# A planned transformer-layer kernel in a new order: DMAs planned with eight lanes, copies of value rows planned after the second x load

## The chip, the cores and the metric

The kernel runs on one core of one Trainium2 chip. The core has five engines with a queue each: TensorE (PE, matmuls), VectorE (DVE), ScalarE (ACT), GpSimd (POOL) and SyncE (SP, which here issues DMAs). The metric is device time in microseconds (us) of one execution. Times below come from three runs of the kernel and from one profiled execution of it.

## The reference

For x of 2048 tokens by 448 channels, bf16:

```python
xn = _layernorm(x, axis=-1)
s = _A_ref(xn, A_wqkv, A_wo)                              # attention
g = _silu(_B_ref(xn, B_w1, B_b1, B_w2, B_b2))             # 448 -> 1792, gelu, -> 448
return x + s * g
# attention: 16 heads of 28; a query at position p sees p, p-2, ..., p-14 (8 keys, step 2)
# softmax over these 8, weighted sum of their values, heads joined, times wo
```

## The kernel before, in words

**Tiles.** Tokens are kept as even ones and odd ones, 16 tiles of 128 tokens, in four chunks of four tiles. The work of a chunk is: load x, statistics (`stats`, L434 and L438 on DVE), reciprocal deviation (`rstds`: for tiles 0 to 3 on ACT and DVE, for later ones two POOL instructions, L455 and L456, over two or four tiles at once), normalised rows (`norm`, L468 on DVE; L482 doubles 64 columns), their transposition (chunk 0 on PE, L492; later chunks by a DMA transpose from SP, `dma_T`, L391), then projections to q and k (`qk_cols`: L583 in chunk 0, L580 later), to values (`vproj`: L619 in chunk 0, inside L510 later) and the first product of the feed-forward part (`ff1`, L510) with its gelu on ACT (L662). Attention is done in nine visits of some 228 queries: scores (L808), exp on ACT (L818), a mask on DVE or POOL (L825), the weighted sum (L841), and four DVE instructions that divide (L852 to L866). The second product `ff2` (L510, at the end L752), its gate (L775 to L785) and the product with wo (L510, at the end L926) close the work with a sum, and SP writes the rows out (L945).

**Copies of value rows.** A visit needs its 128 value rows at other partitions than those where `vproj` left them. `values` (L629) copies them by two or more DMAs issued from POOL (`dma_sb`, L383 to L387), 52 in all, into one of six buffers v0 to v5.

**Last 128 columns of the feed-forward part.** For chunks 1 to 3 they are made by unused columns of the q and k products: `spread` (L1003 to L1018) lays the weights out once, and `moved` (L558) copies 8 rows at a time from qT and kT to a tile hx by DMAs from SP (L567), 16 for a chunk. One gelu on ACT (L673) closes each.

**Halves and nops.** Most products are done by `pair` (L522): two products share the array, 64 rows by 64 columns a matmul. The first half issues 16 matmuls, the second half 12, in swapped places. Between them stands a nop on POOL (L535): it waits for the first half, and the second half waits for it. So a second half on PE can't start before POOL's queue has come to its nop.

**The order.** Nothing is scheduled on the chip. `_Plan` holds a list of tasks, each with an engine, a cost in us, the tasks before it and a priority. `run` (L98) goes through them as a list scheduler with that model of the time and fixes one order for every engine, and `emit` writes the program in that order. DMAs are tasks on an engine named "DMA" of the model, after the issuing instruction. Priorities are tables (`PRIO`, `LATER`, L284 to L306). The order is all that the plan decides: the semaphore waits of the program come from the data that its instructions read and write.

**Lanes.** Every DMA of the program signals its landing on one of eight semaphores, in turn: eight for those that SP and ACT issue, in one sequence, and eight for those of POOL. A DMA is issued only when the one that had its semaphore before has landed. The program before has these waits in it; the plan before knows nothing of them. For example the eighth value copy waits for the landing of b1's load, the ninth for that of the first value copy, and so on.

**POOL's queue around 9 to 20 us, before** (what follows "nop" is what it lets go):

```
copies v0 v0 v0 | nop 1 | copies v1 v2 v1 v2 v2 v2 (the last two wait for a lane) | nop 2 | copy v3 (lane)
| nop 3 | copy v4 (lane) | rstd of tiles 4, 5 | nop 4 | rstd of tiles 6, 7 | nop 5 | copy v5 | nop 6 | copy v3
| three spread copies (L1006) | ...
```

**ACT's and SP's queues, before.** SP issues all early loads: x of tiles 0, 2, 3, the weights of q, k and v, then the first half of w1 (one large, two small DMAs), x of tiles 4 to 7, the second half of w1. Later come four transposes, 16 copies to hx, eight transposes, and so on. ACT issues x of tile 1 early and, between its evacuations of PSUM, x of tiles 8 to 11, the first half of w2, x of tiles 12 to 15 and the second half of w2; in the program before, 8 of SP's hx copies stand between the first and the last of these four in the sequence of lanes.

Of the kernel before, what the change touches and what calls it, by code (L numbers as in the profile page):

```python
# [13 lines left out]
HOP = 0.10  # L14
# [2 lines left out]
SWITCH = 0.095  # L17
BLOCK, FETCH = 128, ((0.0, 5.4), (25.0, 4.0))
SAME = 20
HOPS = ("POOL", "POOL")  # L20
MASK_ON = (("DVE", "POOL"), (0.4, 1.2))

# [9 lines left out]

class _Task:
    __slots__ = ("eng", "cost", "deps", "fn", "prio", "take", "give", "slots",
                 "start", "end", "on", "ndep", "users", "tail", "seq", "table", "limit", "mode", "pairs")


class _Plan:
# [5 lines left out]
        self.tasks = []  # L44

    def add(self, eng, cost, fn, deps=(), prio=0, take=(), give=(), tail=0.0, table=(), limit=None,
            mode=128, pairs=1):
        t = _Task()
        t.eng = eng if isinstance(eng, tuple) else (eng,)
        t.cost = cost if isinstance(cost, tuple) else (cost,) * len(t.eng)  # L50
        t.deps = [d for d in deps if d is not None]
        t.fn, t.prio, t.give, t.tail, t.table, t.limit = fn, prio, give, tail, table, limit
        t.mode, t.pairs = mode, pairs
        t.take = {}
        for p in take:
            t.take[p] = t.take.get(p, 0) + 1
        t.slots = {}
        t.start = t.end = None
        t.on = None
        t.users = []  # L60
        t.seq = len(self.tasks)
        self.tasks.append(t)
        for p in t.take:
            if p.fifo is not None:
                p.fifo.append(t)
        return t

    def _at(self, t, e, free):
        at = free.get(e, 0.0)
        for p, n in t.take.items():  # L70
            if len(p.free) < n or p.fifo and p.fifo[0] is not t:
                return None
            at = max(at, sorted(p.free)[n - 1][0] + HOP)
        if t.table and self.table not in t.table:
            at += TABLE
        for d in t.deps:
            at = max(at, d.end - d.tail if d.on == e else d.end + HOP)
        if e == "PE" and t.mode != self.mode:
            at = max(at, free.get(e, 0.0) + SWITCH)
        return at  # L80
# [17 lines left out]
    def run(self):  # L98
# [4 lines left out]
        free = {}  # L103
        self.table = None
        self.mode, self.issued, self.block = 128, 33, -9.0
        ready = [t for t in self.tasks if not t.ndep]
        order = []
        while ready:
            cand = []
            for t in ready:  # L110
                ways = []
                for e, c in zip(t.eng, t.cost):
                    at = self._at(t, e, free)
                    if at is not None:
                        ways.append((at + (c if len(t.eng) > 1 else 0.0), at, e, c))
                if ways:
                    _, at, e, c = min(ways)
                    cand.append((at, t, e, c))
            if not cand:
                raise RuntimeError("the plan is stuck: " + str([(t.seq, t.eng, t.fn.__qualname__) for t in ready[:20]]))  # L120
            first = min(cand, key=lambda k: k[0])
            near = [k for k in cand if k[2] == first[2] and k[0] <= first[0] + SLACK]
            at, t, e, c = min(near, key=lambda k: (-k[1].prio - self.same(k[2], k[1]),
                                                   k[0], k[1].seq))
            if t.limit is not None and at > t.limit:
                t.fn, c = None, 0.0
            t.on, t.start = e, at
            if e == "PE" and t.fn is not None:
                self.mode = t.mode
                c = self.fetched(at, c, t.pairs)  # L130
            if t.table and self.table not in t.table:
                self.table = t.table[0]
            free[e] = at + c
            t.end = at + c + t.tail
            for p, n in t.take.items():
                got = sorted(p.free)[:n]
                for g in got:
                    p.free.remove(g)
                t.slots[p] = [g[1] for g in got]
                if p.fifo is not None:  # L140
                    p.fifo.pop(0)
            for p, owner, i in t.give:
                p.free.append((t.end, owner.slots[p][i]))
            ready.remove(t)
            order.append(t)
            for u in t.users:
                u.ndep -= 1
                if not u.ndep:
                    ready.append(u)
# [24 lines left out]
def kernel(  # L174
# [87 lines left out]
    def ring(name, n, shape, dt=BF16, fifo=False):  # L262
# [19 lines left out]


    PRIO = {  # L284
        "spread": (-1,),
        "gather": (119, 152.5, 45.5,),
        "qk": (-31, -42, 39.5, 35.5, 17.5, 190, 183.5, 22.5, 124.5, 86, 32, 107.5, 156.5, 104, 142,
            157.5,),
        "values": (52, 145, 24.5, 138.5,),
        "attn": (194, 183, 206, 72.5, 26.5, 16, 45, 78.5, 28,),  # L290
        "ff1": (-56, 2.5, 37.5, 66, 54, 197.5, -17, 14.5, 34.5, 201.5, 19.5, 164, 129.5, 79, 151.5,
            65.5, 16.5, 76, 11.5, 152.5, -15, 138.5, 10, 15.5, 77, 146.5, 142, 70,),
        "gelu": (162, -60, 34.5, 95,),
        "ff2": (2, 101, 1.5, 41, 71, 136, 20, 77, 182, 70.5, 27, 184, 49.5, 6, 17, 16,),
        "final": (20.5, 94.5, 6.5, 113.5, 193.5, 87, 133.5, 38.5, 53.5, 85.5, 0, 20, 5.5, 16, 51.5,
            105,),
        "norm": (50, 8, 97.5, 178.5, 71, 126, 152.5, 51.5, 198.5, 162.5, 89.5, 102, 99, -14.5, 17.5,
            114,),
        "loads": (10, 50, 84.5, 70, 92,),
        "stats": (207.5, 159.5, 110, 199.5, 114.5, 85, 105, 153, 8.5, 4, 95, 95.5, 207, 174, 144.5,  # L300
            85,),
        "turn_x": (27, 181, 74.5, 10.5, 190, 177, 105.5, 75.5, 134.5, 92, 15.5, 88.5, 145, 9.5, 135,
            111,),
        "move_v": (16, 19, 126.5, 47, 183, 104, 197, 195, 126,),
    }
    LATER = {"swap": 92, "qk": 55.5, "v": 108.5, "gelu": 178, "exp": 94.5, "mask": -33.5, "pv": -0.5, "recip": 64, "os": 186, "y": 120.5, "tanh": 33.5, "g": 8, "sg": 78, "o": 146.5}  # L306

    plan = _Plan()

# [64 lines left out]
    def dma(eng, dst, src, kb, prio, deps=(), issue=0.5, rate=350.0, tail=1.7, pieces=1):  # L374
        def fn(_):
            {"SP": nc.sync, "ACT": nc.scalar, "POOL": nc.gpsimd}[eng].dma_start(dst, src)
        a = plan.add(eng, issue, fn, [t_on] + list(deps), prio)
        for _ in range(pieces - 1):
            a = plan.add("DMA", kb / rate / pieces, lambda _: None, [a], prio - 100)
        return plan.add("DMA", kb / rate / pieces, lambda _: None, [a], prio - 100 * (pieces > 1), tail=tail)  # L380


    def dma_sb(dst, src, deps, prio, take=(), give=()):  # L383
        def fn(k):
            nc.gpsimd.dma_start(dst(k), src())  # L385
        a = plan.add("POOL", 0.55, fn, deps, prio, take=take)
        return a, plan.add("DMA", 0.4, lambda _: None, [a], prio, give=give, tail=2.2)  # L387

    def dma_T(dst, src, deps, prio, give, n=1, issue=1.45):
        def fn(_):  # L390
            nc.sync.dma_start_transpose(out=dst, in_=src())  # L391
        a = plan.add("SP", issue, fn, deps, prio)
        return plan.add("DMA", 0.4 + 0.75 * n, lambda _: None, [a], prio, give=(give,) if give else (), tail=1.7)

    t_x = {}

# [161 lines left out]
    def moved(c, which, g, done):  # L558
# [4 lines left out]
        def move(k):  # L563
            hx, of = buf(p_hx, hx_at[c]), (kT if which else qT[:, 0])
            for r in range(2):
                p0 = 64 * which + 16 * g + 8 * r
                nc.sync.dma_start(hx[p0:p0 + 8], of[64 * r + 2 * DH:64 * r + 64, g, c * CH:c * CH + CH])  # L567
        a = plan.add("SP", 1.45, move, [done, hx_at[c]], PRIO["gather"][c - 1])
        t_moved[c].append(plan.add("DMA", 0.15, lambda _: None, [a], PRIO["gather"][c - 1], tail=4.0))

    def qk_cols(which, g, t0, n, prio):
        cs = slice(t0 * P, t0 * P + n)
# [56 lines left out]
    def values(b):  # L629

        t_v[b], v_at[b] = [[], []], []
        for i in range(2):
            first = None
            for w in range(2):
                k0 = VIS[b][2][w][i][1]
                for lo in sorted({k0, max(k0, (k0 + NK - 1) // P * P)}):
# [1 line left out]
                    n = min(k0 + NK - lo, P - r)  # L638
                    at = NK * w + lo - k0
                    a, d = dma_sb(lambda k, f=first, at=at, n=n: buf(p_v, f or k)[at:at + n], lambda t=t, r=r, n=n: v_tok[t][r:r + n],  # L640
                                  t_vt[t] + [first], PRIO["move_v"][b], () if first else (p_v,))
                    first = first or a
                    t_v[b][i].append(d)
                    v_used[t + 8].append(d)
# [286 lines left out]
    def close(t, cs, n, gated, own, i, a, prio):  # L931
# [11 lines left out]

        def f4(_):
            nc.sync.dma_start(rows(o_half, t * P, P)[:, cs], buf(p_o, o)[:, :n])  # L945
        q = plan.add("SP", 0.55, f4, [o], 50)
        plan.add("DMA", 0.4, lambda _: None, [q], 50, give=((p_o, o, 0),), tail=1.2)

    for t in range(TPC):
        stats(t)  # L950
# [170 lines left out]
```

## Time and profile before

| | |
|---|---|
| three runs | 160.75, 159.84, 160.93 us (median 160.75) |
| profiled execution | 160.16 us |
| its span, first to last instruction | 158.4 us |
| PE busy | 149.8 us (95%) |
| DVE busy | 117.1 us (74%) |
| ACT busy | 97.2 us (61%) |
| POOL busy | 59.1 us (37%) |
| mean granted PE clock | 0.993 |

In the profile, L510 is line 510 of the program before. An engine name with q (POOLq, ACTq, SPq) is its sequencer: a nop, a wait or the issue of a DMA. "A <- B" says that A waited and that B ended the wait. Two different matmuls on quarters of the array run at the same time, so 16 of them with 512 columns each take about as long as four on the whole array, though the profile gives each 0.38 us.

### The profile page before, as it was taken

The numbers are of one execution on the slowest core, as the hardware profiler recorded it, in microseconds if no ns is written. First come the engines' busy times: TensorE is split into PE (matmuls) and PEld (weight loads), VectorE is DVE, ScalarE is ACT, GpSimd is POOL, SyncE is SP. The second block draws the span as 40 slices with busy tenths as digits, with TensorE's granted clock in tenths as the row PEclk, the third lists the DMA queues.
The fourth block names the chain that finished last, engine by engine and source line by source line (L and its number), as shares of the span: only waits on it lengthen the run. The fifth ranks groups of instructions, "written<-read, shape, count | busy, mean of one in ns | idle before, by whom it ended". The sixth has DMA issues, their size and how long they took to land.

```text
span 158.4 us, 7839 instructions
## 1 busy us (share of the span) xinstructions
PE 149.8 (95%) x3409; PEld 100.7 (64%) x3409; DVE 117.1 (74%) x272; ACT 97.2 (61%) x177; POOL 59.1 (37%) x115
## 2 busy tenths in 40 slices
PE   6997799999899999999999999999999999999980
PEld 2543555556546656776778777675996986776480
DVE  6860980166259377999999899999939999169882
ACT  3474589850879777677876328873486587920220
POOL 7165771626036305227008985265003870000000
PEclk9999999999999999999999999999999999999997
DMA  5999865238827964202002532035020200001121
GB/s 143 276 278 315 205 97 97 53 82 278 256 91 139 126 76 101 58 12 53 4 8 75 160 95 68 19 108 154 11 62 4 62 4 4 0 4 32 55 65 32
DMA packets 19476, 14.92 MB, mean 94 GB/s; under 512 B 10422, under 2 KB 18660, under 8 KB 19441
## 3 DMA queue, kind: packets, MB, share of 16 engines
q1 hardware_dynamic: 13968, 7.59, 21.2%
q0 software_dynamic: 2368, 4.06, 10.1%
q10 hardware_dynamic: 3104, 2.75, 5.7%
q8 instruction: 27, 0.44, 1.2%
q14 instruction: 9, 0.07, 0.1%
HBM read 7.06 MB, written 1.84 MB: 56 GB/s over the span
## 4 chain that ended last, share of the span: by engine, by line
PE 79%; DVE 9%; DMA 7%; issue 1%; ACT 1%; ACTq 0%; SPq 0%; POOL 0%; DVEq 0%; POOLq 0%
PE bank L510 56%; PE bank L580 6%; DMA v<-v_tok 4%; PE bank L752 3%; PE bank L841 3%; PE bank L339 3%; DMA hx<-qT 3%; PE bank L583 2%; DVE qT L598 2%; PE bank L808 2%; DVE E L825 1%; DVE dt L861 1%; DVE g L785 1%; DVE xnT L866 1%; DVE dt L852 1%
## 5 line engine op out<-in xcount | busy, mean ns | idle before, releaser
L510 PE MATMUL bank<-xnT,w 64*64 64x512 bf16 (+1 forms) x784 | 43.0, 365 | 1.0 <-ACT v_tok L324 0.8
L385 POOL DMA_DIRECT2D v<-v_tok x52 | 28.1, 543 | 34.5 <-PE bank L841 13.3
L510 PE MATMUL bank<-w,h_all 64*64 64x448 bf16 x744 | 39.6, 349 | 0.0
L662 ACT ACTIVATE h_all<-bank,b 128x512 bf16<-128x512 f32 (+1 forms) x56 | 32.9, 669 | 7.9 <-PE bank L510 7.9
L510 PEld LDWEIGHTS <-w 64*64 64x64 bf16 x784 | 25.2, 107 | 16.5 <-issue 1.6
L510 PEld LDWEIGHTS <-h_all 64*64 64x64 bf16 x744 | 26.6, 107 | 7.5 <-issue 0.4
L596 ACT ACTIVATE qT<-bank,own 128x512 bf16<-128x512 f32 (+1 forms) x26 | 15.9, 655 | 10.6 <-PE bank L583 3.7
L580 PE MATMUL bank<-xnT,wqk 64*64 64x512 bf16 x336 | 21.3, 377 | 0.0
L825 POOL TENSOR_TENSOR E<-E,m_gen 128x456 bf16<-128x456 bf16 (+1 forms) x13 | 13.6, 1057 | 20.1 <-ACT E L818 17.3
L818 ACT ACTIVATE E<-bank 128x456 bf16<-128x456 f32 (+1 forms) x36 | 16.9, 555 | 5.2 <-PE bank L808 5.2
L781 ACT ACTIVATE t<-y 128x448 f32<-128x448 f32 x15 | 8.6, 583 | 17.2 <-DVE y L775 17.2
L852 DVE STREAM_TRANSPOSE dt<-bank 128x480 f32<-128x480 f32 (+1 forms) x18 | 12.1, 671 | 5.2 <-PE bank L841 5.1
L580 PEld LDWEIGHTS <-wqk 64*64 64x64 bf16 x336 | 10.8, 107 | 6.5 <-issue 0.4
L434 DVE BATCH_NORM_STATS2 st<-x_sb 128x6 f32<-128x448 bf16 x16 | 9.7, 611 | 4.5 <-DMA x_sb<-in_A_x_dram 4.5
L510 PEld LDWEIGHTS <-xnT 64*64 64x64 bf16 x296 | 10.0, 107 | 4.3
L861 DVE STREAM_TRANSPOSE dt<-rd 128x480 f32<-128x480 f32 (+1 forms) x18 | 12.1, 675 | 0.6
L825 DVE TENSOR_TENSOR E<-E,m_gen 128x456 bf16<-128x456 bf16 x19 | 8.5, 479 | 2.5 <-ACT E L818 2.4
L598 DVE TENSOR_SCALAR qT<-bank,own 128x512 bf16<-128x512 f32 x8 | 5.8, 747 | 5.5 <-ACT qT L596 4.2
L324 ACT CAST v_tok<-bank 128x448 bf16<-128x448 f32 x10 | 5.2, 534 | 6.9 <-PE bank L510 5.3
L468 DVE TENSOR_SCALAR xn<-x_sb,mv,rstd 128x448 bf16<-128x448 bf16 x15 | 6.0, 400 | 4.2 <-POOL rstd L456 3.2
L775 DVE TENSOR_TENSOR y<-bank,b 128x448 f32<-128x448 f32 x15 | 8.7, 616 | 0.4 <-PE bank L752 0.4
L510 PE MATMUL bank<-w_v,xnT 64*64 64x448 bf16 x144 | 8.8, 349 | 0.0
(96 smaller groups left out, 196.0 us busy)
## 6 DMA issues: line engine op xcount, KB each, us to landing
v<-v_tok POOLq DMA_DIRECT2D x20, 96.0 KB, 3.2
out_dram<-o SPq DMA_DIRECT2D x15, 112.0 KB
w<-in_B_w_dram ACTq DMA_DIRECT2D x2, 784.0 KB
w<-in_B_w_dram SPq DMA_DIRECT2D x2, 672.0 KB
x_sb<-in_A_x_dram ACTq DMA_DIRECT2D x2, 448.0 KB
h_all<-in_A_wqkv_dram SPq DMA_DIRECT2D x4, 168.0 KB
w<-in_B_w_dram SPq DMA_DIRECT2D x4, 112.0 KB
x_sb<-in_A_x_dram SPq DMA_DIRECT2D x1, 448.0 KB
```

The source lines that it names most:

```text
L385: nc.gpsimd.dma_start(dst(k), src())
L434: nc.vector.bn_stats(out=buf(p_st, k)[:], in_=x_sb[:, t, :])
L510: return [lambda c=c: nc.tensor.matmul(out[c:c + n], lhsT[:, c:c + n], rhs, start=start, stop=stop) for c in range(0, P, n)]
L580: return [lambda i=i: nc.tensor.matmul(ps[64 * i:64 * i + 64, :n], w[:, i], xnT[r, kt, cs], start=start, stop=stop) for i in range(2)]
L596: nc.scalar.activation(qT[:, z, g, cs], buf(p_b, o, i)[:, :n], ACT.Copy, scale=own[:, z:z + 1])
L598: nc.vector.tensor_scalar(qT[:, z, g, cs], buf(p_b, o, i)[:, :n], own[:, z:z + 1], None, op0=ALU.mult)
L662: nc.scalar.activation(buf(*at)[:, c0:c0 + n], buf(p_b, own, i)[:, :n], ACT.Gelu_apprx_tanh, bias=b1[:, mt:mt + 1])
L775: nc.vector.tensor_tensor(out=buf(p_y, k)[:, :n], in0=buf(p_b, own, i)[:, :n], in1=b2[:, cs], op=ALU.add)
L818: nc.scalar.activation(buf(p_E, k)[:, :n], buf(p_b, a, hl)[:, :n], ACT.Exp, scale=SCALE)
L825: (nc.gpsimd if k.on == "POOL" else nc.vector).tensor_tensor(out=E, in0=E, in1=m[:, :, :nq], op=ALU.mult)
L852: nc.vector.transpose(buf(p_dt, k)[:, :32 * m], buf(p_b, po, w)[:, :32 * m])
L861: nc.vector.transpose(buf(p_dt, d)[:, :32 * m].rearrange("p (b c) -> p b c", c=32), buf(p_rd, r)[:, :m].unsqueeze(2).to_broadcast((P, m, 32)))
```

## The change

The plan is given the lanes. Each task carries the number of DMAs it issues (`issues`), and the task on the model's DMA engine that ends with their landing (`land`). `_at` lets a task start no earlier than the landing of the DMA eight before it in its sequence (SP and ACT, or POOL). Transposes and hx copies get other model costs, and `values` names the load of x tiles 4 to 7 as a task that comes before every value copy. No instruction is told to wait for that load by this: it acts on the order alone. All priorities are other numbers.

```diff
+LANES = 8
...
+        for i in range(t.issues):
+            sent = self.sent[e == "POOL"]
+            if len(sent) + i >= LANES:
+                last = sent[len(sent) + i - LANES]
+                if last.end is None:
+                    return None
+                at = max(at, last.end + HOP - 0.6 * i)
...
+            self.sent[e == "POOL"].extend([t.land] * t.issues)
...
-    def dma_T(dst, src, deps, prio, give, n=1, issue=1.45):
+    def dma_T(dst, src, deps, prio, give, n=1, issue=1.3):
...
-        return plan.add("DMA", 0.4 + 0.75 * n, lambda _: None, [a], prio, give=(give,) if give else (), tail=1.7)
+        a.land = plan.add("DMA", 0.4 + 0.75 * n, lambda _: None, [a], prio, give=(give,) if give else (), tail=1.3)
...
-        a = plan.add("SP", 1.45, move, [done, hx_at[c]], PRIO["gather"][c - 1])
-        t_moved[c].append(plan.add("DMA", 0.15, lambda _: None, [a], PRIO["gather"][c - 1], tail=4.0))
+        a = plan.add("SP", 1.3, move, [done, hx_at[c]], PRIO["gather"][c - 1], issues=2)
+        a.land = plan.add("DMA", 0.15, lambda _: None, [a], PRIO["gather"][c - 1], tail=2.4)
...
+        later = [t_x[TPC + 3]]
...
-                                  t_vt[t] + [first], PRIO["move_v"][b], () if first else (p_v,))
+                                  t_vt[t] + [first] + later, PRIO["move_v"][b], () if first else (p_v,))
```

(The tables `PRIO` and `LATER` are replaced number by number.) The matmuls are the same 3409. What moves in the built program, engine by engine:

- PE: in chunk 0 the first q and k product and its second half come before the last two transposes; the first two pairs of `ff1` come before the other three and a half q and k pairs, which come interleaved with `ff1`. Values, q and k of chunk 1 are taken between pairs of `ff1` of chunk 0. From the last `ff1` chunk on, the order is the one before.
- POOL's queue at the same place as above, after:

```
nop 1 | copies v0 v0 | nop 2 | copy v0 | nop 3 | copies v1 v2 | rstd of tiles 4, 5 | nop 4 | copy v2 | nop 5
| copies v2 v2 | rstd of tiles 6, 7 | nop 6 | copy v3 (lane) | nop 7 | copies v3 v1 v4 (lanes) | nop 8 | ...
```

- DVE: the three spread copies move from POOL to DVE, between the statistics of tiles 7 and 6, and one more comes from ACT; it takes 11 of the 34 evacuations of qT instead of 8, most of them early.
- ACT: gelu starts after chunk 0's first q and k product; the loads of x tiles 8 to 15 and of w2 are issued between the first gelus. In the sequence of lanes all four come right after the four transposes of chunk 1, before any hx copy.
- SP: the same 93 DMAs; two rows of output and some hx copies change places.

## Prediction, made before the change was run

> **What bounds the kernel now.** I read the shares of engines first, then the waits of PE, the chain that ended last, and PE's busy time by stretches.
>
> ```profile
> PE 149.8 (95%) x3409; PEld 100.7 (64%) x3409; DVE 117.1 (74%) x272; ACT 97.2 (61%) x177; POOL 59.1 (37%) x115
> ```
>
> PE is busy for 149.8 of 158.4 us, and the change leaves its matmuls alone. So it can only win what PE stands still, or lose by new stalls. The waits of PE tell where it stands:
>
> ```profile
> PE bank L583 <- POOLq L535: 1.8, 1, 1.8
> PE bank L339 <- DVE eps_t L331: 1.2, 1, 1.2
> PE bank L510 <- ACT v_tok L324: 0.8, 1, 0.8
> PE bank L510 <- POOLq L535: 0.2, 1, 0.2
> ```
>
> The 1.2 us is the start. The other three can be followed in the chain (start, length, what):
>
> ```profile
> 9.13 6.96 DMA v<-v_tok
> 16.09 0.02 issue
> 16.11 0.02 POOLq L385
> 16.13 0.49 issue
> 16.62 0.03 POOLq L535
> ...
> 33.45 0.75 DVE qT L598
> 34.20 0.13 SPq L567
> 34.33 0.06 issue
> 34.39 4.77 DMA hx<-qT
> 39.16 0.02 issue
> 39.18 0.38 ACTq L376
> 39.55 0.04 issue
> 39.60 0.54 ACT v_tok L324
> 40.14 0.04 issue
> 40.18 5.01 PE bank L510 x87
> ```
>
> First: the first value copy takes 6.96 us to land amid the loads; the ninth copy waits for its lane; nop 2 stands behind the ninth copy; PE waits for nop 2. Second: ACT's issue of x tiles 12 to 15 waits 4.77 us for the lane of an hx copy, and behind it stands the evacuation that PE needs. Both are lane waits, which the new plan knows.
>
> PE's busy time by stretches confirms that little else is to be had:
>
> ```profile
> 14.00:15.00 1.00, 0.85 (x16) 0.23 (x8) 0.00 (x0) 0.34 (x2) 0.00 (x0) 1.00 1.07 275
> 15.00:16.00 1.00, 0.00 (x0) 0.00 (x0) 0.12 (x1) 0.00 (x0) 0.00 (x0) 1.00 1.08 264
> 16.00:17.00 1.00, 0.31 (x8) 0.21 (x12) 0.97 (x3) 0.00 (x0) 0.36 (x1) 1.00 1.18 277
> 38.00:40.00 2.00, 1.42 (x28) 0.76 (x21) 1.19 (x3) 0.40 (x1) 0.46 (x1) 1.00 0.67 205
> 40.00:42.00 2.00, 1.82 (x36) 1.29 (x39) 0.00 (x0) 1.56 (x4) 0.00 (x0) 1.00 0.71 197
> ```
>
> (Columns: length; busy PE, weight loads, DVE, ACT, POOL; clock; DMA share; GB/s.) PE idles 1.84 us in 14 to 17 and 0.76 us in 38 to 42; from 48 to 152 us all of it is 0.15 us.
>
> **The change, part by part.** Unit: 16 matmuls of 512 columns on quarters take 0.86 us, 12 take 0.65 (chain: 152 in 8.20 us, 54 ns each).
>
> *A. Opening.* Up to the second group of L619, ending at 9.15, both orders are the same. New order from there: q and k half 0.57 (10.05 to 10.62 before), its second half 0.33, two transpositions 0.90 together, two groups of L619 at 0.96 each, b1's 0.07: 12.9. Then `ff1`, whose weights land at 13.2 by the trace's landing events: 13.25. Two pairs of `ff1` are 2 x 0.86 + 2 x 0.65 = 3.0 (16.3; only three value copies of 0.54 stand before nop 3, so nops 2 and 3 come in time), then two q and k first halves, 1.7: 18.0. There PE needs nop 4, and in the new POOL order rstd of tiles 4 and 5 stands ahead of it. Before, that chain ran from the landing of x tiles 4 to 7 (DVE's statistics start at 15.88) to the end of rstd at 19.44: three statistics, then 0.31 and 0.72 on POOL, 3.56 us. The landing may move a little: up to 15.86 the POOL queue had moved 190 KB, of which the new order has issued 127 KB; 63 KB at 275 GB/s are 0.2 us. So nop 4 at 15.65 + 3.6 = 19.25, and PE idles 1.25 us. The stall of 1.84 is replaced, not removed. By 19.25 PE has done 102 units of 54 ns of chunk 0 (46 of q and k, 56 of `ff1`); before, it had done 128 at 21.32. The missing 26 take 1.4: 20.65. **-0.65.** Bounds: -0.45 (x lands as before) to -1.9 (x lands by 14.4, no wait). (The Trainium skill, "DMA: Bandwidth & Descriptors", section "Anatomy of one DMA — SWDGE (gpsimd) path", prices a copy from POOL at 2.0 us and its bytes at 436 GB/s: 2.2 us for these 96 KB, an estimate. By that the first lane would have been free at 12.0, two us before the ninth copy, and there would be no stall to remove; the trace has 6.96 us and a stall, and it decides.)
>
> *B. Spread copies on DVE.* These now stand in DVE's queue between statistics of tiles 7 and 6 and wait for the last of w1; behind them the statistics of tile 6, then rstd of tiles 6 and 7 on POOL, then nop 6, which PE needs at 19.25 + 2 x 0.65 + 2 x 0.86 = 22.3. The last of w1 landed at 20.33 before, held up by 650 KB of value copies in 13 to 20 us; by then the new order has issued about half, so I take 18.3. DVE: third statistics 18.0; copies as long as on POOL (0.51, 0.29, 0.24), 19.0; 0.62 statistics, two rows with doubling 1.18, 0.18: 21.0; rstd 1.12: nop 6 at 22.2. **+0.1.** Bounds: 0 and +1.4 (w1 as late as before: 23.7).
>
> *C. Loads on ACT.* All four lanes are now those of early loads and none of an hx copy, so the 4.77 us wait has no source, and the loads go out from about 25 to 31 us instead of 29.6 to 39.6. What is late next are hx copies that wait for lanes of these loads: SP's fifth hx copy for x tiles 8 to 11, its sixth to eighth for the other three. They end well ahead of the gelu over hx. **-0.76.** Bounds: -0.76 and 0 (the wait moves to that gelu).
>
> *D. Third wait.* At 45.2 PE waited 0.20 us for a nop behind rstd of tiles 8 to 11 (0.31 + 1.05 us). In the new order such a nop stands there too, x is earlier. **-0.1.** Bounds: -0.2 and 0.
>
> *E. Transposes of chunk 1.* DVE gets early evacuations of qT (0.75 each), and one of kT (0.66), between the rows of tiles 6 and 7: after rstd, 22.2, two rows 0.40 each, 0.19 of doubling, 0.75, 0.66, then the last doubling, some 25.2 to 25.5. The fourth transpose lands 4.1 us after SP starts it (before: 24.2 to 28.26): 29.6. PE reaches the first L580 at about 29.55 (22.3 plus 110 units of 54 ns and 28 matmuls of 448 columns at 48). Before there was a margin of 1.1 us, now none. **+0.1.** Bounds: 0 and +2.5, the trace showing nothing of DVE's new queue.
>
> *F. The rest.* 50 to 115 us is reordered, with the same operations (one mask of 1.07 us moves from POOL to DVE at 0.48); the last stretch keeps its order. With 0.15 us of idle PE nothing is to be won; DVE is at 3.8 to 3.9 of 4 us in 60 to 84, so a misplaced evacuation would cost. **0.** Bounds: -0.5 and +0.8.
>
> Sum: -0.65 + 0.1 - 0.76 - 0.1 + 0.1 = -1.3. The profiled execution took 160.16 (span 158.4, 1.76 around it): 158.85. It lies 0.59 below the median of the runs, 160.75, and 0.26 below the mean of all four times, 160.42; I allow part of that: **159.0**.
>
> **The rivals.**
>
> 1. *No new stall at nop 4.* If fewer value copies let x tiles 4 to 7 land by 14.4, A gives -1.9: 157.7. For: bytes of the hardware queue in 13 to 16 us fall from 321 to 182 KB per us as the POOL queue's grow from 47 to 80. Against: until 13 us only loads move, and x still needs its 2.8 MB ahead of it. 0.20.
> 2. *Gain given back at nop 6 (B).* w1 lands as late as before, 1.4 us stall: 160.3. For: value copies still overlap it. Against: half as many. 0.18.
> 3. *Slower: DVE makes the transposes late (E).* Place: the first L580. It decides from 1.3 us on, where the whole gain is gone; at 2.5 us it gives 161.5. For: DVE's new queue, with 3.83 us of 4 busy already in 16 to 20. Against: 4 idle us in 24 to 28 before. 0.12.
> 4. *A long stall halves PE's clock.* The trace shows PE slow after idleness: the warm-up matmuls of L339 take 4.88 us for 5632 columns, 0.87 ns each, later ones 0.42. If x landed at 17.9, the stall at nop 4 would be 3.5 us: 161.3 from the wait alone, and about 163.0 if the next 3.5 us ran at that rate. The longest idle time before is 1.84, with no slowing behind it. 0.02. (The Trainium skill, "TensorE: Matmul & The Clock Gate", section "What's actually happening", puts the switch at an idle window of about 3.4 us; the trace agrees as far as it goes, 1.84 us being under it, while the profile's clock column says 1.00 at the slow start too.)
> 5. *The change does not do what it says.* No semaphore makes copies wait for x; the order alone does, and two copies still go out at about 10 us. This is in A already; the lane waits of POOL move behind nop 6, by when lanes are free.
>
> **How the numbers follow.** Main case 0.48, with 158.2 to 159.9; rivals 0.20, 0.18, 0.12, 0.02. About 1% is what a measurement of this kernel tells from no change. Faster than 159.14: 0.28 of the main case and rival 1, 0.48. Slower than 162.36: rival 4 and the far part of rival 3, which with losses in F could reach it, 0.08. Between: 0.44. The range reaches from rival 1 with 0.5 won in F to a little short of rival 3's 161.5: 157.2 to 161.3; outside it lie about 0.05 below and 0.12 above.
>
> **What would show it.** A: PE's wait at L583 for the nop, released by rstd, 1.25 us near 18 to 19 us, in place of 1.84; no lane wait on POOL before it. B: no wait of PE for the nop at 22 us. C: the wait of PE for v_tok's evacuation gone, ACT's four loads issued by about 31 us. D: no wait near 45. E: none at the first L580, or a short one for the DMA of xnT. F: PE idle under 0.3 us from 50 us on. It would be wrong if DVE came late in 18 to 26 us, or if PE waited between 50 and 115 us.

## The result, and the profile after

| | before | after |
|---|---|---|
| eight runs each, median | 160.50 us (159.84 to 160.93) | 163.82 us (161.74 to 167.40) |
| ratio | | 1.0121, 95% interval 1.008 to 1.0162 |
| profiled execution | 160.16 us | 161.74 us |
| its span | 158.4 us | 159.9 us |

Medians here are over all runs of a kernel and ratios leave out the longer ones: of the eight runs after, four had a mean granted clock of 0.964 to 0.988 and took 164.3 to 167.4 us, and the ratio is over the other four, 161.74 to 163.34. The forecast was 159.0, 157.2 to 161.3: wrong in its sign. The span grew by 1.5 us.

The line numbers are those of the new kernel, 9 to 14 higher: its L522 is L510 of before, L593 is L580, L596 is L583, L402 the transpose of L391, L385 the load of L376. Shares of the engines:

```profile
PE 149.1 (93%) x3409; PEld 101.3 (63%) x3409; DVE 120.9 (76%) x280; ACT 95.7 (60%) x173; POOL 57.5 (36%) x111
```

PE is busy 0.7 us less than before, and the span is 1.5 us longer, so PE stands still some 2.2 us more. Where, the waits of PE tell (who waited for what: us in total, times, longest):

```profile
PE bank L593 <- DMA xnT<-xn: 3.4, 1, 3.4
...
PE bank L522 <- DMA xnT<-xn: 0.7, 1, 0.7
PE bank L504 <- DVE xn L480: 0.6, 2, 0.4
```

Nothing is left of the waits for a nop (1.8 and 0.2 us) and for v_tok (0.8 us) that were to go. In their place PE waits 3.37 and 0.72 us for transposes of chunk 1. PE's busy time by stretches, at the places shown of before and at the new hole (columns as there; the last row is the kernel before):

```profile
16.00:17.00 1.00, 1.00 (x24) 0.54 (x20) 0.64 (x3) 1.00 (x3) 0.97 (x3) 1.00 0.34 91
38.00:40.00 2.00, 2.00 (x44) 1.30 (x36) 1.42 (x3) 1.16 (x2) 1.39 (x3) 1.00 0.43 118
```

```profile
24.00:28.00 4.00, 3.28 (x72) 1.82 (x68) 0.77 (x2) 1.08 (x3) 2.89 (x12) 1.00 0.99 238
28.00:32.00 4.00, 1.27 (x24) 0.51 (x16) 2.85 (x9) 1.77 (x4) 0.91 (x4) 1.00 1.18 208
32.00:36.00 4.00, 3.35 (x68) 2.42 (x72) 0.12 (x1) 0.84 (x2) 0.00 (x0) 1.00 0.95 321
...
24.00:28.00 4.00, 4.00 (x80) 2.18 (x76) 0.00 (x0) 4.00 (x7) 0.60 (x1) 1.00 0.53 100
```

The old holes are closed, and a new one is open from 29.27 to 32.65 us, with the DMA engines full (share 0.99 to 1.18; before it was 0.53 in 24 to 28 us). The chain that ended last (start, length, what) passes through it:

```profile
16.34 3.88 PE bank L596 x72
20.22 0.86 PE bank L522 x16
...
23.86 0.11 DVE xn L494
23.97 0.02 issue
23.99 8.52 DMA xnT<-xn
```

The rows of the last transpose are ready at 23.97 us. SP starts it at once, and it takes 8.52 us to land, where the last of before took 4.0 (24.30 to 28.26). Some copies from POOL move beside it in both kernels; what is new beside it is on ACT's queue (start, length, DMA; first after, then before):

```profile
22.44 0.41 ACTq L385 DMA_DIRECT2D x_sb<-in_A_x_dram  x1
22.89 1.01 ACTq L385 DMA_DIRECT2D w<-in_B_w_dram  x1
...
29.58 0.37 ACTq L376 DMA_DIRECT2D x_sb<-in_A_x_dram  x1
34.23 0.37 ACTq L376 DMA_DIRECT2D w<-in_B_w_dram  x1
```

ACT issues x of tiles 8 to 11 (448 KB) at 22.4 and the first half of w2 (784 KB) behind it, at 22.9: 1.5 and 1.1 us before the rows of the last transpose are ready. Before, these two went out at 29.58 and 34.23, when the transposes had landed. In the plan the four loads stand behind the issue of the four transposes, at 24.6 us of its time; but that acts on the order alone, nothing on the chip makes ACT wait for SP, and ACT came to them 2.2 us earlier than planned. The plan's transpose, moreover, lands 0.4 + 0.75 + 1.3 = 2.45 us after its turn on the model's one DMA engine; a load never makes it longer.

**Theory.** The loads, which the change moved ahead of the transposes, crowd them out; it costs the two waits of 4.1 us together and eats the gains of A, C and D. **Rivals.** DVE's new queue made the rows late (the prediction's own rival); POOL's copies crowd the transposes; the loss is spread over the rest.

### The profile page after: what moved, and what is told of

Its sections match the earlier page's. It is cut to its first block, busy times and chain, and to the rows that moved or that the text cites. A ratio compares the mean times of both kernels' runs of the same rounds, so it can differ in the third digit from the quotient of the medians.

```text
span 159.9 us, 7831 instructions
## 1 busy us (share of the span) xinstructions
PE 149.1 (93%) x3409; PEld 101.3 (63%) x3409; DVE 120.9 (76%) x280; ACT 95.7 (60%) x173; POOL 57.5 (36%) x111
## 3 DMA queue, kind: packets, MB, share of 16 engines
HBM read 7.06 MB, written 1.84 MB: 56 GB/s over the span
## 4 chain that ended last, share of the span: by engine, by line
PE 71%; DVE 15%; DMA 8%; issue 1%; SPq 1%; ACT 1%; DVEq 0%; ACTq 0%
PE bank L522 48%; PE bank L593 9%; DMA xnT<-xn 5%; PE bank L766 3%; PE bank L596 3%; PE bank L855 3%; DMA x_sb<-in_A_x_dram 3%; DVE dt L875 2%; DVE dt L866 2%; PE bank L822 2%; DVE sg L949 2%; DVE o L955 2%; DVE xnT L880 1%; PE bank L632 1%; SPq L385 1%
## 5 line engine op out<-in xcount | busy, mean ns | idle before, releaser
L522 PE MATMUL bank<-xnT,w 64*64 64x512 bf16 (+1 forms) x784 | 43.1, 365 | 0.0
L676 ACT ACTIVATE h_all<-bank,b 128x512 bf16<-128x512 f32 (+1 forms) x56 | 33.0, 667 | 10.9 <-PE bank L522 10.6
L522 PE MATMUL bank<-w,h_all 64*64 64x448 bf16 x744 | 38.9, 349 | 0.0
L522 PEld LDWEIGHTS <-w 64*64 64x64 bf16 x784 | 25.7, 107 | 13.6
L522 PEld LDWEIGHTS <-h_all 64*64 64x64 bf16 x744 | 25.2, 107 | 8.1
L593 PE MATMUL bank<-xnT,wqk 64*64 64x512 bf16 x336 | 20.8, 377 | 3.5 <-DMA xnT<-xn 3.4
L609 ACT ACTIVATE qT<-bank,own 128x512 bf16<-128x512 f32 (+1 forms) x23 | 14.7, 678 | 14.9 <-PE bank L593 11.9
L839 POOL TENSOR_TENSOR E<-E,m_gen 128x456 bf16<-128x456 bf16 (+1 forms) x14 | 14.9, 1080 | 17.0 <-ACT E L832 14.7
L593 PEld LDWEIGHTS <-wqk 64*64 64x64 bf16 x336 | 11.4, 107 | 9.5 <-issue 3.8
L522 PEld LDWEIGHTS <-xnT 64*64 64x64 bf16 x296 | 10.5, 107 | 5.3 <-DMA xnT<-xn 1.2
L611 DVE TENSOR_SCALAR qT<-bank,own 128x512 bf16<-128x512 f32 (+1 forms) x11 | 7.2, 672 | 6.6 <-ACT qT L609 6.5
L522 PE MATMUL bank<-w_v,xnT 64*64 64x448 bf16 x144 | 9.1, 350 | 0.7 <-DMA xnT<-xn 0.7
L839 DVE TENSOR_TENSOR E<-E,m_gen 128x456 bf16<-128x456 bf16 (+1 forms) x18 | 7.2, 423 | 3.3 <-ACT E L832 3.0
L855 PEld LDWEIGHTS <-v 64*64 64x64 bf16 x576 | 7.5, 108 | 1.4 <-issue 0.4
```

The lines of the kernel that those rows point to most:

```text
L522: return [lambda c=c: nc.tensor.matmul(out[c:c + n], lhsT[:, c:c + n], rhs, start=start, stop=stop) for c in range(0, P, n)]
L593: return [lambda i=i: nc.tensor.matmul(ps[64 * i:64 * i + 64, :n], w[:, i], xnT[r, kt, cs], start=start, stop=stop) for i in range(2)]
L609: nc.scalar.activation(qT[:, z, g, cs], buf(p_b, o, i)[:, :n], ACT.Copy, scale=own[:, z:z + 1])
L676: nc.scalar.activation(buf(*at)[:, c0:c0 + n], buf(p_b, own, i)[:, :n], ACT.Gelu_apprx_tanh, bias=b1[:, mt:mt + 1])
L839: (nc.gpsimd if k.on == "POOL" else nc.vector).tensor_tensor(out=E, in0=E, in1=m[:, :, :nq], op=ALU.mult)
L855: nc.tensor.matmul(banks[w][64 * r:64 * r + 64, c0:c0 + nq], v[rs, 2 * g + r, 32 * z:32 * z + 64], E[rs, c1:c1 + nq], start=(i, g, z) == ( ...
```

## Experiments

All move DMAs in the finished order and leave the plan as it is, by this edit; the times are those of the plan, and a task behind a moved one follows it:

```diff
     plan.run()
+    x8, w2a, w2b, x12 = 324, 331, 342, 353
+    move = {...}
+    for t in plan.order:
+        t.start = move.get(t.seq, t.start)
+        t.start = max([t.start] + [d.start for d in t.deps])
+    plan.order.sort(key=lambda t: (t.start, t.seq))
```

**1. The changed kernel, loads later.**

```diff
+    move = {x8: 29.1, w2a: 29.12, x12: 29.14, w2b: 29.16}
```

> The changed kernel, with the four ACT loads (x 8-15, w2; 2464 KB) put behind the sixth gelu of chunk 0 in ACT's queue, so that they go out at about 29.5 us instead of 22.4 to 29.6. Theory (loads issued at 22.4 us crowd out the transposes of chunk 1): the last two transposes land by 28.5 us instead of 29.9 and 32.5, PE's waits for xnT (3.4 at L593, 0.7 at L522) fall under 0.5 together, and the time is 161.7 - 3.7 = 158.0 us, 157.3 to 158.8. Rival (DVE's rows are late): rows are ready when they were, the wait of 3.4 stays, 161.7. Rival (value copies or b2 from POOL crowd them): the wait stays above 2.5, above 160.5. Rival (the loss is spread over the rest): the wait goes, but the time stays above 160.

Measured: 159.14 us, just above the expected 157.3 to 158.8, ratio to the kernel before 0.9907 (0.9869 to 0.9945). Of the ten runs seven lie at 157.9 to 159.7 and three at 161.5 to 162.3. The loads went out from 28.7 us; by the landing events the last two transposes landed at 27.21 and 27.65. Waits of PE, in a run of 161.51:

```profile
PE bank L593 <- issue: 1.5, 1, 1.5
...
PE bank L522 <- DMA xnT<-xn: 0.5, 1, 0.5
```

No wait for the last transpose is left (the 1.5 us are another place, at 62 us, and taken up below). The 0.5 us at L522 are for the second transpose, where the changed kernel waited 0.7: that wait is there without the loads too, so they account for the 3.4 us at L593 and at most 0.2 of the other. The rivals that leave the wait at L593 where it is have fallen: the rows and copies were left as in the changed kernel, and only the loads were moved.

**2. Only the second load and those behind it later.**

```diff
+    move = {w2a: 29.12, x12: 29.14, w2b: 29.16}
```

> The changed kernel, with only w2 and x 12-15 put behind the sixth gelu; x 8-11 (448 KB) still goes out at 22.4 us. Theory by bytes (1232 KB in flight beside the transposes cost 4.4 us of landing time): 448 KB cost about a third, the last transpose lands at 29.2 to 30, PE's wait is 0 to 1 us, 158 to 159.5. If any load beside them is enough, whatever its size: wait above 2.5, above 160.5.

Measured: 159.21 us, 0.9909 (0.987 to 0.9949), as expected. The last transpose landed at 29.75 and PE waited 0.40 us for it. With 448 KB beside it the transpose lands 2.1 us later than with none, which PE's margin nearly covers. So the 784 KB of w2 are the larger part of the harm.

**3. The kernel before, loads earlier.** Is crowding enough by itself, in the old order of DVE and PE?

```diff
+    move = {x8: 21.86, w2a: 21.862, x12: 28.78, w2b: 28.79}
```

> The kernel before, with x 8-11 and the first half of w2 issued by ACT ahead of its first gelu (about 22.5 us instead of 29.6 and 33) and x 12-15 and the other half at about 29.6. The order of everything else stays. Theory (crowding is enough by itself): the last transpose lands at about 32 instead of 28.26, PE waits 2 to 3 us at the first L580, the lane wait of 4.77 us on ACT is gone (-0.76), 161.5 to 163. Rival (the new order of DVE and PE made the wait, not the loads): no wait at L580, 159.4.

Measured: 161.22 us, just under the expected 161.5 to 163, 1.0034 (0.9996 to 1.0072): the time alone does not tell it from no change. The waits of PE do:

```profile
PE bank L580 <- DMA xnT<-xn: 2.6, 1, 2.6
PE bank L583 <- POOLq L535: 1.7, 1, 1.7
```

The last transpose landed at 31.92 instead of 28.26. The wait for v_tok (0.8 us) was gone, which offsets a part. The new wait appeared in a kernel that had none of the change but the place of the loads.

**4. The kernel before, value copies later** (term A alone).

```diff
+    move = {198: 20.8, 202: 20.8, 204: 21.6, 206: 21.6, 208: 23.92, 292: 23.92}
```

> The kernel before, with six of its value copies moved in POOL's queue behind the rstds and nops of chunk 0 (five copies stay early, as in the changed kernel). Nothing else moves. Theory (crowding by copies held x and w1 back, and the ninth copy's lane held nop 2): x 4-7 lands at 13.5 to 14.5 instead of 15.86, the wait of 1.84 at L583 is gone and not replaced by one behind rstd, 160.2 - 1.8 = 158.4, 157.9 to 159.0 for a profiled run. Rival (the stall is only replaced by one of some 1.2 us behind rstd, as my prediction had it): 159.5 to 160.

Measured: 160.27 us, 0.9987 (0.9954 to 1.0021): no gain, outside what the theory expected. Yet the wait at L583 was gone: x of tiles 4 to 7 landed at 14.04, w1's second half at 19.39, and PE was 1.6 us earlier than before from 16 us on. The time was given back behind it. Waits of PE:

```profile
PE bank L580 <- ACT E L818: 1.1, 1, 1.1
PE bank L510 <- ACT v_tok L324: 0.8, 1, 0.8
```

The wait for v_tok is the one of before, and PE comes out of it still 1.6 us earlier (38.55 against 40.18). ACT waits for the lane of an hx copy as before (5.03 us in the chain, ending at 38.57 against 39.16), and behind that 0.4 us are lost by 44 us. The other 1.3 are lost at L580, where PE arrives early and starts at 56.90 against 56.83 before. The view names exp on ACT there, but exp is not late. PE's group and the exps in this run, then the same two in the kernel before, and a wait of DVE in this run:

```profile
56.90 3.22 PE L580 MATMUL bank<-xnT,wqk 64*64 64x512 bf16 x56 [1.14 <-ACT E L818]
54.90 1.88 ACT L818 ACTIVATE E<-bank 128x456 bf16<-128x456 f32 x4
...
56.83 3.19 PE L580 MATMUL bank<-xnT,wqk 64*64 64x512 bf16 x56
56.15 1.88 ACT L818 ACTIVATE E<-bank 128x456 bf16<-128x456 f32 x4
...
56.79 0.40 DVE L468 TENSOR_SCALAR xn<-x_sb,mv,rstd 128x448 bf16<-128x448 bf16 x1 [1.15 <-DMA xnT<-xn]
```

Before, PE's group starts 0.7 us after the exps do and waits for nothing; here it starts 2.0 us after them. A group of L580 also needs the transposes of its chunk, and the last of chunk 2 landed at 56.76 here, against 55.49 before; DVE waits for a transpose to the same moment. So most of A's gain is lost in this profile behind a transpose that came no earlier; why it landed late is not shown.

**5 and 6. The kernel before, loads in the middle, without and with later copies** (term C, and A with C).

```diff
+    move = {x8: 28.78, w2a: 28.782, x12: 28.784, w2b: 28.786}
```

> The kernel before, with its four ACT loads (x 8-15, w2) issued together at about 29.6 us, after the transposes of chunk 1 have landed and ahead of all hx copies in the sequence of lanes. Nothing else moves. This is term C of the prediction alone: ACT's lane wait of 4.8 us has no source, PE's wait of 0.76 for v_tok is gone. Theory (C as predicted): 160.16 - 0.8 = 159.4 profiled, ratio 0.995. Rival (2464 KB at once delay the hx copies or x 8-11, and the wait moves): no gain, 160 to 160.5.

> The kernel before with both edits: six value copies later (as in copies_late) and the four loads at about 29.6 us (as in loads_mid). copies_late won 2.1 us before 20 us and lost it again, 0.8 at the lane wait of ACT and 1.1 at 57 us, where ACT, held up by that wait, was late with exp. Theory (the gain of A was given back through C's wait, so the two together win more than the sum of both alone): 160.2 - 1.9 - 0.8 = 157.5, 157.0 to 158.3, ratio 0.980 to 0.987. Rival (ACT is the bound at 57 us by its own work): the wait at 57 us stays, 158.5 to 159.5.

Measured: the loads alone 158.92 us, 0.9895 (0.9833 to 0.9957), better than expected; both 159.30 us, above the expected 157.0 to 158.3, 0.9875 (0.9814 to 0.9936). In the profile of the first only the wait at L583 is left after the start; in that of the second (157.28 us, span 155.6) not even that, and no wait of PE after the start is over 0.33 us. The transpose of chunk 2 that cost experiment 4 its gain landed at 54.07 and 53.10. Both kernels beat those of before and after. But the runs of the second lie at 157.3 and 157.7 and at 159.2 to 159.6, so it ran again, once alone for a profile and once beside the loads alone:

> The same kernel as copies_and_loads, for one more profile: its runs lay at 157.3 and 157.7 and at 159.2 to 159.6, and the profile had caught 157.28. Theory (one of the 16 parts of a transpose lands some 2 us after the others, behind a 16 KB fetch of instructions, as in the profiles of w2_late and loads_late): if this execution is of the upper group, it shows a wait of PE of 1 to 2 us for xnT behind such a part. Rival (a part of the early loads is late): the wait lies before 20 us.

> The same kernel as copies_and_loads (both edits on the kernel before), beside loads_mid on one chip, to size term A once C's wait is gone: the profiles differ by 1.5 us of span (157.1 and 155.6), the medians by less. Theory (A is worth its 1.6 us stall as soon as C's wait no longer takes it back): median 157.2 to 158.2, 1.0 to 1.7 below loads_mid. Rival (in most runs something behind the opening takes it back): median 158.9 to 159.5, no lower than loads_mid.

> The same kernel as loads_mid (the loads alone): 158.8 to 159.5 as before, if the chip is like the last one.

Measured: the single execution took 157.00 us and had no wait of PE over 0.12 us after the start, so it tells nothing of the upper group. Together on one chip: both edits 158.60 us, 0.9859 (0.9811 to 0.9907; without the two longest of six runs), in runs of 157.5 to 157.9 and 159.3 to 160.1; the loads alone 158.92 us, 0.9917 (0.9889 to 0.9946). The median of both edits lies between what theory and rival had expected. Of 13 runs of both edits six lie at 157.0 to 157.9, some 1.4 below the loads alone; seven lie at 159.2 to 160.1, no lower than the loads alone. So A is worth about its stall in some runs and nothing in others. What takes it back there no profile caught; it stays open.

**7. The changed kernel, all four loads early** (twice the bytes).

```diff
+    move = {x12: 25.15, w2b: 25.16}
```

> The changed kernel, with x 12-15 and the second half of w2 issued right behind the first two loads, at about 24 us instead of 28.5: 2464 KB beside the transposes instead of 1232. Theory (landing time of the last transpose grows with the bytes beside it: 27.65 us with none, 29.75 with 448 KB, 32.51 with 1232): 34 to 36 us, PE's wait at L593 5 to 7 us, 164 us and more. Rival (transposes have a share of their own, and only the first DMAs matter): 32.5, wait 3.4, 161.7. If an idle PE of over 3.4 us lowers its clock, the granted clock is below 0.99 in every run here, and the profile shows where.

Measured: 167.03 us, 1.0367 (1.0298 to 1.0436), clock 0.975 to 0.990 in all four runs. Waits of PE:

```profile
PE bank L593 <- DMA xnT<-xn: 6.3, 1, 6.3
```

The last transpose landed at 37.64. The theory had the direction and said 34 to 36. The dose, by landing of the last transpose: 27.65 us with no load beside it, 29.75 with one, 32.51 with two, 37.64 with four. Counted from SP's start of that transpose, since SP did not start it at the same time in all four: 3.2, 5.2, 8.5 and 12.3 us, one execution each.

**8 and 9. The changed kernel, with work in the hole** (is it idleness that lowers the clock in half of its runs?).

```diff
             p, q = buf(p_b, k, 0), buf(p_b, k, 1)
+            for _ in range(8 if k.seq == 270 else 0):
+                nc.tensor.matmul(p[:, :CH], w1[:, 0, :P], w1[:, 0, :CH], start=True, stop=True)
```

> The changed kernel, with eight matmuls of 512 columns (some 1.7 us at 0.21 each), whose result is overwritten, ahead of the group at L593 for which PE waits 3.4 us; they need nothing that is late. Half of the runs of the changed kernel had a mean clock of 0.964 to 0.988 and took 164.3 to 167.4 us. Theory (PE idle for about 3.4 us lowers its clock in a part of the runs): with the idle time cut in two, no run has a clock below 0.99 and the median is 161.7 to 162.5. Rival (the clock falls for another reason): as many runs below 0.99 as without, median near 163.8.

Measured: 166.59 us, 1.0363 (1.032 to 1.0407), clock 0.974 to 0.990 in all six runs: against the theory as I had put it. But the experiment did not make the hole smaller. ACT's third load went out at 27.84 instead of 28.47, the last transpose landed at 34.74 instead of 32.51, and PE was idle for 4.3 us behind the added matmuls. Stretches of that profile:

```profile
33.00:34.00 1.00, 0.00 (x0) 0.00 (x0) 0.00 (x0) 0.00 (x0) 0.00 (x0) 0.83 1.03 175
34.00:35.00 1.00, 0.21 (x4) 0.19 (x8) 0.00 (x0) 0.00 (x0) 0.00 (x0) 0.50 1.07 324
...
40.00:41.00 1.00, 1.00 (x20) 0.58 (x16) 0.74 (x2) 0.54 (x2) 0.00 (x0) 0.75 0.03 8
```

The clock falls to 0.50 while PE is idle and stays there until 40.5. The next run had sixteen matmuls:

> The changed kernel, with sixteen instead of eight overwritten matmuls of 512 columns ahead of the group at L593 (some 3.4 us). With eight, PE stopped at 30.5 us, the last transpose landed at 34.74, PE was idle for 4.3 us and its granted clock was 0.50 from 33.7 to 40.5 us; 166.6 us. Theory (the idle time, not the lateness, lowers the clock): idle time is 4.3 - 1.7 = 2.6 us, the clock stays at 1.00, no run below 0.99, and the time is 166.6 less half of 6.8 us: 163.2, 162 to 164. Rival (the clock falls for another reason, such as the load of the DMAs): clock 0.975 and 166.6 again.

Measured: 164.75 us, 1.0159 (1.0087 to 1.0231); three of six runs have a clock of 0.984 to 0.990 and took 165.5 to 167.1 us, the others one of 0.994 to 1.000 and 162.1 to 164.0. In its profile (165.5 us) there is no idle time at L593, and the clock is 1.00 there. But it fell elsewhere, behind a wait of 2.2 us for the second transpose:

```profile
27.00:28.00 1.00, 0.58 (x8) 0.37 (x12) 0.00 (x0) 0.00 (x0) 0.00 (x0) 0.67 0.90 216
28.00:29.00 1.00, 1.00 (x17) 0.45 (x12) 0.00 (x0) 0.00 (x0) 0.00 (x0) 0.50 1.14 290
...
30.00:31.00 1.00, 1.00 (x16) 0.48 (x12) 0.00 (x0) 0.55 (x1) 0.76 (x5) 0.63 1.07 245
31.00:32.00 1.00, 1.00 (x32) 0.70 (x24) 0.72 (x2) 0.89 (x3) 0.81 (x4) 1.00 1.16 287
```

In the profiles of experiments 7 to 9 the clock fell at a hole of PE, and where the hole is filled it holds. The load of the DMAs is not the cause: their share is 1.07 to 1.16 in the two slices from 30 to 32 us, while the clock rises to 1.00, and 1.18 in the changed kernel's hole, with a clock of 1.00. The expected time came in the three runs without a lower clock; that the other wait was short in these is likely, but no profile caught one.

## Why the prediction was wrong, point by point

**E failed, and with it the sum.** The step that failed is "The fourth transpose lands 4.1 us after SP starts it". It landed 8.52 us after (by the start in the trace, 24.30, the figure of before is 4.0). The rows were not late: 23.97 against 25.2 to 25.5 in the forecast, so that with 4.1 us PE would have had a margin of over a microsecond at 29.27. The 4.1 us came from a stretch (24 to 28 us before) with a DMA share of 0.53; in the new order the share is 0.99 to 1.18. E costs 4.1 us (both waits) instead of 0.1. Experiments 1, 2, 3 and 7 put the 3.37 at L593 down to the loads; of the 0.72 for the second transpose, 0.48 are left with the loads moved away (experiment 1).

**C was right and had a price that the prediction did not see.** The lane wait went, and with it PE's 0.76. But it took the loads to go out "from about 25 to 31 us"; they went out at 22.4 to 29.6. And to what is late next it answered the hx copies; it was the transposes. It is one move with two ends: at about 29 us it wins (0.9895 and 0.9917, more than the 0.76 us it was put at), at 22.4 it loses all of it and more.

**A had the right sign and was mis-sized:** -1.84 (PE has no idle time from 12 to 24 us) instead of -0.65. x of tiles 4 to 7 landed at 13.44 us, not 15.65, and rstd was done before PE asked. That is the first rival, whose condition was 14.4. How much of the earlier landing the copies make is not settled: x landed at 13.4 to 14.9 in the ten profiles with two to five copies started before it, and at 14.38, 14.71, 15.60 and 15.86 in the four with eight, so it varies by over a microsecond with the copies unchanged. With eight, PE waited 1.5 and 1.6 us at nop 2 even with x there at 14.7 and 14.4: that stall is the lane's, as the prediction read it. Experiment 4 adds that A is not a term of a sum: alone its 1.6 us were taken back, 0.4 behind C's lane wait and 1.3 behind a transpose of chunk 2.

**B and D came as forecast.** No wait at nop 6, as w1 landed at 16.8, before the 18.3 taken; no wait near 45 us. (Of the copies that held up w1 before, B took 650 KB in 13 to 20 us; by the packets it is 760.)

**F:** the waits over 0.1 us after 50 us are 0.47 us instead of 0.12, and PE is busy 0.7 us less, so the rest gave about nothing. Another 0.65 us of idle time lies before 10 us, behind x of tiles 2 and 3 landing 0.9 us later; the profile of experiment 1, with the same order there, has none of it.

In numbers, against the profiled execution of before: A -1.84, C -0.76, D -0.20, E +4.09, start +0.65, F +0.35 - 0.7 in PE's busy time. That makes +1.6; the profiled execution is 1.58 us longer. Without E the sum is -2.5, below the forecast of -1.3; with the loads moved back the ratio of 0.9907 is some -1.5, so a part of the 2.5 is not there in most runs.

**The rivals.** The third named the place, the first q and k group of chunk 1 (L580 before, L593 after), and nearly the time (161.5), but a wrong cause (DVE). The fourth had 2 in 100 and a place that never idled; its mechanism is there all the same, in the profiles of experiments 7 to 9. The changed kernel's runs with a clock of 0.964 to 0.988 fit it, but no profile caught one of them. If they are its work, the change costs more than the ratio says: the medians, 163.82 and 160.50, differ by 2.1%.

## What to carry to other kernels

When a wait on an issuing engine goes, ask not only what is won but when the DMAs behind it now start, and what short transfer with a reader waiting is in flight then; a landing time from the old trace holds only for the traffic it was measured in. A dependence in a planner orders instructions on one engine, and two engines that share nothing but the DMA engines will not keep it; put the bulk load behind an instruction of its own queue that comes surely after the transfer has landed. And test a term alone and with the others: what one stall gave up can be lost at the next thing that is late, so two terms are not a sum. Where a view puts a wait down to an engine that is no later than before, look for a DMA that is.

## What the runs showed of the hardware

**Small transposes beside large loads.** The last transpose of chunk 1 took 4.0 us to land in the profile of before, and 8.5 and 10.6 beside loads of 448 and 784 KB that another engine had issued (the changed kernel, and experiment 8). That SP's queue held nothing else did not help. The Trainium skill, "DMA: Bandwidth & Descriptors", section "Queues, rings and completion order", says that each DMA engine takes turns between the queues with work, a packet at a time. The traces agree so far as the transposes do land before the loads beside them are through (32.51 against 35.03 for w2). That more loads delay it more does not speak against equal turns by itself: in experiment 2 the one load was through at 27.53, before the transpose at 29.75. But in experiments 7 and 8 the third load was issued earlier, behind a second that was still under way, and the transpose took 12.3 and 10.6 us instead of 8.5; turns between the two queues alone would not make that. With one execution each, this stays open.

**One part of a transpose behind a fetch of instructions.** The 1.5 us at L593 in experiment 1 and 1.3 us at the same place in experiment 2 have no releaser in the profile. The landing events show it: of the sixteen parts of the last transpose of chunk 3, fifteen land together and one some 2 us later. Each time a fetch of 16 KB of PE's instructions (queue q8) starts 2.0 to 2.4 us before that late part:

```
                       15 parts by   last part   fetch starts
loads_late                  60.58       62.23         60.04
w2_late                     58.89       61.00         59.01
w2_late, earlier one        48.92       50.48         48.45
after                       51.59       53.06         51.03
before                      23.14       24.55         22.26
loads_early                 23.17       24.71         22.35
```

Only in the first two did PE wait for it. The two profiles of the kernel of experiment 5 show it twice more (fetch at 22.07 and 21.45, last part at 24.37 and 23.75). That the two go together was seen in these eight cases; no experiment moved the fetch, so the cause is not shown.

**The granted clock.** PE's clock fell to half behind 4.3 and 6.3 us of idleness for 6.8 us each (0.34 + 6 + 0.5 from the rows of experiment 8), behind 2.2 us for 3.4 (0.66 + 2 + 0.74, experiment 9), and not at all behind 3.37 us in the changed kernel's profile nor 1.84 before. The Trainium skill, "TensorE: Matmul & The Clock Gate", section "What's actually happening", has a window of about 3.4 us that runs freely and an idle one lowers the clock. The lengths of one and two such windows agree, and so do all stretches at full clock: from the first clock record on, each lasts a whole number of steps of 3.413 us in all fourteen traces. The steps also sort the cases that the length of a pause does not. In each of the 17 falls, those after the last matmul included, PE was busy for 0 to 37% of the step before it (37% in experiment 9, where nearly the whole pause of 2.2 us lies in one step). In no other step at full clock was it busy for less than 41%: 41% in the changed kernel, whose pause of 3.37 us is cut by the border of two steps, and 42% in experiment 3. So here the clock fell by the busy share of a step, with a border between 37 and 41%; it was found in the traces afterwards, and no run was made to try it.
